# Two outer products of the first unit, M3 and M4, by two Strassen levels instead of one

## The chip, the cores and the metric

The kernel runs on one core of a Trainium2 chip. A core has a matrix engine (TensorE, "PE" in the profile, with its weight loads as "PEld"), a vector engine (VectorE, "DVE"), a scalar engine (ScalarE, "ACT"), a general engine (GpSimd, "POOL") and a queue engine (SyncE, "SP") that issues most transfers; 16 DMA engines move data. TensorE writes only to PSUM, which has eight banks here (tags `g1`, `g3`, `s0`, `s1`, `q01`, `q02`, `q11`, `q12`), each of 128 partitions by 512 numbers of float32. The metric is the time of one execution in microseconds (us), the median of several runs.

## The reference

The kernel computes a linear attention and feeds it to four experts whose results are summed by gates:

```python
# attention: 4 batches, 8 heads, 768 positions, 64 wide, in blocks of 64
intra = ((qb @ kb.T) * Dmask) @ vb
inter = (qb * lam_pow) @ kv_state
out[:, :, sl] = intra + inter
kv_state = lam_block * kv_state + (kb * rev_pow).T @ vb
...
x = attention_out                      # 3072 tokens x 512
p = domain_probs / (domain_probs.sum(-1, keepdims=True) + 1e-09)
for e in range(4):
    h = np.maximum(x @ w1[e], 0.0)     # 3072x512 @ 512x1024
    out += p[:, e:e + 1] * (h @ w2[e]) # 3072x1024 @ 1024x512
```

All is float32.

## The kernel before

The tokens are cut into three groups of 1024 (`g`), and a unit is one group with one expert, twelve in all. In each unit the first product `x @ w1[e]` and the second product `h @ w2[e]` are done by Strassen's scheme in Winograd's form: seven products M1 to M7 of sums of weight blocks (`A_OF`: A11, A12, A22 and the sums S1 to S4) with sums of token blocks (`B_OF`: B11, B21, B22 and T1 to T4). These seven are the outer products.

From the second unit on, each outer product of the first product is split once more by the same scheme (`first_product`): seven inner products of two matmul instructions, 128 x 256 each. For it the weight block is cut in four, and four inner sums (named S3, S1, S2, S4 again, `S_OPS`) are made by GpSimd into a tile `ops`; the token block is cut in four too, and four inner sums are made in place in `xs` (`x_steps`). The inner products go in the order M1, M7, M6, M4, M5, nothing, M3, M2 (`FIRST`). M1, M6, M5 and M3 add into one bank (`g1`), M7, M4 into another (`g3`), which is then taken anew for M2 and filled ahead with an earlier result by ScalarE (`seed`). After each of them VectorE or ScalarE reads the running sum out of the bank, adds what came earlier, and leaves a block of the result.

The first unit (group 0, expert 0) is different. Its token blocks come straight from the attention of group 0, which runs at the same time, and its outer products are done without the second split (`direct_product`, L1547 to L1585): four quarters of four matmul instructions, each quarter with a bank of its own. M6, M7 and M4 add into the same four banks (`chains`), so that M4's quarters hold M6 + M7 + M4. M7 and M4 need only a Relu after an addition of M5 and of M1. The order is M1, M2, M5, M6, M7, M3, M4 (`SEQ0`).

Since the inner weight sums of expert 0 are not used in the first unit, GpSimd makes them later, in the chores of `prepare_w1(0)`, and stores them in `w1_ops` in DRAM for groups 1 and 2, where `feed` loads them. The sums of expert 1, for the second unit, are made ahead of each outer product (`own_w1`), used from SBUF and stored too.

The order of the instructions on each engine is the order in which the program writes them. A planner decides on that: `now` counts steps of the main loop, `busy`, `moved`, `asked`, `filled` are its estimates of how far GpSimd, the DMA engines, SP and VectorE are booked. `pump` takes the next chore (`chores`: loads, weight sums) when these allow it, and sends stores (`queue`) some steps after their sums. `own_sums` holds VectorE's inner sums of the token blocks, of which one is taken at a step. An outer product that needs what has no entry yet makes the planner take it by force.

Tiles rotate: `stage` has seven buffers of 128 x 1024 for weight blocks and sums, `small` tiles of 128 x 512 come from a pool of 42. A tile that takes a used buffer waits for the last reader of that buffer. Each transfer signals on one of eight semaphores in turn, and one issued on a semaphore waits for the earlier one on it.

While M6, M7, M3 and M4 of the first unit run, VectorE also makes the sums of the token blocks (`x_sums`), the gates (`gates`, L578 to L600, four operations on VectorE and seven copies on ScalarE) and the inner sums of unit 1's first token block (`own_x("M1")`). The other inner sums of unit 1's token blocks are made in unit 1. GpSimd makes the sums of expert 0's and then expert 1's second weights (`prepare_w2`, tiles `w2b` and `w2o`), and the first weights of expert 1 (`w1b`, `w1o`, `ops`).

Of the kernel before, what the change touches and what calls it, by code (L numbers as in the profile page):

```python
# [12 lines left out]
ALU = mybir.AluOpType  # L13
# [8 lines left out]
def kernel(  # L22
# [233 lines left out]
    def weight_steps(block, total, ready):  # L256
        return [
            lambda: (block("A11", 0, 0), block("A21", 1, 0), block("A22", 1, 1)), pause(6),
            lambda: ready("M1"),
            lambda: total("S1", "A21", "A22", ALU.add), lambda: ready("M5"),  # L260
            lambda: total("S3", "A11", "A21", ALU.subtract), lambda: ready("M7"),
            lambda: (block("A12", 0, 1), total("S2", "S1", "A11", ALU.subtract)), lambda: ready("M6"),
            lambda: ready("M2"),
            lambda: total("S4", "A12", "S2", ALU.subtract), lambda: ready("M3"),
            lambda: ready("M4"),
        ]

    def prepare_w1(e):
        st = {}

        def block(name, i, j):
            t = stage.tile([P, 2, W], FP32, name="w1b", tag="st")
            src = moe_w1[e, j * 256:(j + 1) * 256, i * W:(i + 1) * W]
            send(out=t[:], in_=src.rearrange("(c p) f -> p c f", p=P))
            st[name] = t

        def total(name, a, b, op):
            t = stage.tile([P, 2, W], FP32, name="w1o", tag="st")
            halves(t[:], st[a][:], st[b][:], op)
            st[name] = t  # L280

        def ready(m):
            inner_w1(e, m, st[A_OF[m]])

        return weight_steps(block, total, ready)
# [768 lines left out]
    def first_product(g, e, m, blocks, tags):  # L1054
# [3 lines left out]
        while unit_of[g, e] in (1, 2 * E) and to_do.get(m):  # L1058
            take(own_sums, True)
# [444 lines left out]
    def own_w1(m):  # L1504

        c = w1_now[1][A_OF[m]]
        b = {f"A{i + 1}{j + 1}": c[j][:, i * 256:(i + 1) * 256] for i in range(2) for j in range(2)}
        s = stage.tile([P, 4, 256], FP32, name="ops", tag="st")
        for n, x, y, op in S_OPS:
            b[n] = s[:, SLOT[n]]  # L1510
            tt(nc.gpsimd, b[n], b[x], b[y], op)
        store(keep_own(("w1", 1, m), w1_ops[1, MS.index(m)], (
            ((0, 1), c[0][:, 0:256].unsqueeze(1)), ((1, 5), s[:]), ((5, 7), c[1].rearrange("p (a f) -> p a f", a=2)),
        )[slice(1, 2) if A_OF[m][0] == "A" else slice(0, 3)]))
        return {i: b[A_OF[i]] for i in A_OF}
# [8 lines left out]

    def own(m):
# [7 lines left out]
    ADDED = {"M1": None, "M2": "M1", "M5": "M1", "M6": "M5", "M7": "M5", "M3": "M6", "M4": "M1"}  # L1533

    def direct_product(m, blocks, tags):
# [4 lines left out]
        def quarter(at, part=None):  # L1540
# [4 lines left out]
            elif m in ("M2", "M6", "M7", "M4"):  # L1545
# [7 lines left out]
            for s in range(2) if part is None else (part,):  # L1553
                f = i * 256 + s * P
                for c in range(2):
                    nc.tensor.matmul(  # L1556
                        out=p[:, s * 256:(s + 1) * 256], lhsT=a[c][:, f:f + P], rhs=b[:, c, j * 256:(j + 1) * 256],
                        start=(s == 0 and c == 0 and m not in ("M2", "M7", "M4")), stop=True, skip_group_check=True,
# [4 lines left out]
            new[at] = blocks[old][at] if m in ("M7", "M3", "M4") else small("m" + at)  # L1563
# [7 lines left out]
            if m in ("M3", "M7", "M4"):  # L1571
                nc.scalar.activation(out=new[at][:], in_=new[at][:], func=AF.Relu)

# [81 lines left out]
    def sum_own(name, a, b, op=ALU.subtract):  # L1655
# [14 lines left out]
    for m in SEQ0[2:]:  # L1670
# [3 lines left out]
        work = direct_product(m, blocks, ("g1", "g3")) if m != "M5" else [m5[1], *m5[3:]]  # L1674
# [38 lines left out]
    for at, (g, e) in enumerate(units):  # L1713
# [15 lines left out]
        for i in range(7):  # L1729
# [36 lines left out]
            if at == i == 0:  # L1766
                for m in SEQ[1:]:
                    own_x(m)
# [73 lines left out]
```

## Time and profile before

The time before is 1155.02 us, the median of three runs (1154.9 to 1155.08).

| what | value |
|---|---|
| profiled execution, its own time | 1158.15 us |
| its span, first to last instruction | 1156.3 us |
| TensorE clock granted | 1.000 |
| TensorE busy | 1143.0 us (99%) |
| VectorE busy | 790.0 us (68%) |
| ScalarE busy | 369.8 us (32%) |
| GpSimd busy | 771.4 us (67%) |
| data moved | 269.22 MB, 233 GB/s |
| first unit's M6 and M7 on TensorE | 59.88 to 73.84 us |
| first unit's M3 | 73.84 to 80.75 us |
| first unit's M4 | 80.75 to 87.65 us |
| second unit's first matmul | 87.65 us |

A row of a group of instructions gives: line, engine, operation, tiles written <- tiles read, shape, count | busy time in us, mean time of one in ns | idle time of the engine just before them and what ended it. A row in order of time gives: start in us, length in us, engine, line, operation, tiles, shape, count, and in brackets the idle time before and what ended it. In a table of stretches a row gives the stretch, its length, then for PE, PEld, DVE, ACT and POOL the busy us and the count, the TensorE clock, the busy share of the DMA engines and GB/s. In the chain, a row is start, length and what the chain went through. The line of nearly every tensor_tensor operation is that of a helper (L117), so the tiles tell which it is: `pc` and `pM` are banks of the first unit's direct products, `pg` of two-level products, `q` of second products, `m` are blocks of results, `xs` token blocks, `ops` inner weight sums, `w1o` and `w2o` outer weight sums, `w1b` and `w2b` raw weight blocks. TensorE runs a float32 matmul instruction as two records.

### The profile page before, as it was taken

The page shows a single profiled execution, that of the slowest core. Times are in us where ns is not written, and L with a number is a line of the kernel's source. Part 1 is how long each engine was busy: PE and PEld are TensorE (multiplying, and loading weights), DVE is VectorE, ACT ScalarE, POOL GpSimd, SP SyncE. Part 2 cuts the span into 40 slices and gives each one's busy share as a digit, 9 for nine tenths or more (in the row PEclk, how much of TensorE's full clock was granted, in tenths as well). Part 3 has the DMA queues.
Part 4 walks back from the last instruction along what each step waited for, and adds up shares of the span by engine and source line. Part 5 has one row for each costly group of instructions (what it writes and reads, how often), then busy time and mean ns, then how long its engine had stood idle before and what let it go on. Part 6 is the DMA issues. An engine that isn't in the chain of part 4 may idle for free.

```text
span 1156.3 us, 22167 instructions
## 1 busy us (share of the span) xinstructions
PE 1143.0 (99%) x8015; PEld 990.3 (86%) x8015; DVE 790.0 (68%) x1428; ACT 369.8 (32%) x746; POOL 771.4 (67%) x732
## 2 busy tenths in 40 slices
PE   8999999999999999999999999999999999999998
PEld 7788888888888888888888888888888888888887
DVE  5576775477477757835775567989765566776785
ACT  4322133223312221222243442243354442342332
POOL 2748318647742974874784998894995783873884
PEclk9999999999999999999999999999999999999999
DMA  8796667999899999895957669966777756657552
GB/s 192 175 281 190 175 191 230 310 292 285 280 302 315 275 287 300 268 349 178 296 186 243 193 201 284 311 226 203 219 241 248 219 167 198 195 162 210 171 191 74
DMA packets 309148, 269.22 MB, mean 233 GB/s; under 512 B 141424, under 2 KB 244016, under 8 KB 309040
## 3 DMA queue, kind: packets, MB, share of 16 engines
q1 hardware_dynamic: 291360, 262.66, 74.0%
q10 hardware_dynamic: 17648, 5.15, 2.0%
q8 instruction: 64, 1.05, 0.4%
q14 instruction: 44, 0.36, 0.1%
q0 software_dynamic: 32, 0.00, 0.0%
HBM read 194.83 MB, written 77.10 MB: 235 GB/s over the span
## 4 chain that ended last, share of the span: by engine, by line
PE 87%; DVE 5%; POOL 3%; issue 1%; DMA 1%; SPq 1%; ACT 1%; DVEq 0%; POOLq 0%; ACTq 0%
PE pg L1096 37%; PE pq L1454 20%; PE q L1155 20%; DVE m L117 2%; PE pM L1556 2%; PE pc L1556 2%; POOL acc L117 1%; DVE sums L117 1%; PE sp L721 1%; PE op L775 1%; POOL ops L117 1%; DVE xs L117 1%; PE sp L728 1%; PE op L793 1%; SPq L114 1%
## 5 line engine op out<-in xcount | busy, mean ns | idle before, releaser
L1096 PE MATMUL pg<-xs,ws_in 128*128 128x256 f32 x1960 | 473.0, 381 | 3.7 <-DVE m L117 3.5
L1096 PEld LDWEIGHTS pg<-xs,ws_in 128*128 128x128 f32 x1960 | 369.0, 190 | 59.5 <-DVE m L117 9.5
L117 DVE TENSOR_TENSOR m<-pg,m 128x512 f32<-128x512 f32 x374 | 255.4, 686 | 104.1 <-PE pg L1096 92.0
L1155 PE MATMUL q<-w2t,m 128*128 128x256 f32 x1120 | 265.7, 380 | 0.5 <-DVE m L117 0.5
L1155 PEld LDWEIGHTS q<-w2t,m 128*128 128x128 f32 x1120 | 212.1, 190 | 29.9 <-DVE m L117 1.1
L117 POOL TENSOR_TENSOR m<-m,decay 128x512 f32<-128x512 f32 x91 | 115.4, 1283 | 89.4 <-ACT m L1113 74.0
L117 DVE TENSOR_TENSOR sums<-pq,sums 128x256 f32<-128x256 f32 x272 | 112.9, 421 | 85.5 <-PE pq L1454 75.8
L1454 PE MATMUL pq<-acc,w2t 128*128 128x256 f32 x688 | 169.3, 379 | 0.0
L1454 PEld LDWEIGHTS pq<-acc,w2t 128*128 128x128 f32 x688 | 130.7, 190 | 17.8
L1113 ACT ACTIVATE m<-m 128x512 f32<-128x512 f32 x99 | 62.4, 630 | 191.2 <-DVE m L117 191.0
L117 DVE TENSOR_TENSOR m<-m,m 128x512 f32<-128x512 f32 x112 | 103.4, 923 | 6.0 <-ACT m L1079 5.9
L1173 DVE SCALAR_TENSOR_TENSOR acc<-q,gate,acc 128x256 f32<-128x256 f32 x108 | 52.0, 481 | 73.9 <-PE q L1155 73.7
L1109 ACT COPY m<-pg 128x512 f32<-128x512 f32 x88 | 51.6, 586 | 123.8 <-PE pg L1096 119.4
L1073 ACT COPY pg<-m 128x512 f32<-128x512 f32 x77 | 45.4, 589 | 133.3 <-DVE m L117 118.7
L117 POOL TENSOR_TENSOR acc<-hT,hT 128x512 f32<-128x512 f32 x56 | 71.2, 1287 | 18.2 <-PE pq L1454 15.7
L117 POOL TENSOR_TENSOR acc<-hT,acc 128x512 f32<-128x512 f32 x56 | 71.3, 1273 | 8.5 <-PE pq L1454 4.7
L1454 PE MATMUL pq<-hT,w2t 128*128 128x256 f32 x288 | 70.0, 379 | 0.0
L117 POOL TENSOR_TENSOR w2o<-w2b 128x512 f32<-128x512 f32 x26 | 35.5, 1386 | 49.0 <-DMA w2b<-in_moe_w_dram 44.5
L1454 PEld LDWEIGHTS pq<-hT,w2t 128*128 128x128 f32 x288 | 54.5, 190 | 7.6
L1454 PE MATMUL pq<-m,w2t 128*128 128x256 f32 x228 | 55.5, 380 | 0.0
L928 ACT COPY hp<-m 128x512 f32<-128x512 f32 x84 | 48.4, 589 | 16.0 <-DVE hT L117 15.0
L117 POOL TENSOR_TENSOR xs<-xs 128x256 f32<-128x256 f32 x28 | 23.8, 849 | 44.5 <-DMA xs<-x_blocks 42.8
(149 smaller groups left out, 1438.4 us busy)
## 6 DMA issues: line engine op xcount, KB each, us to landing
w2t<-w_ops SPq DMA_DIRECT2D x129, 256.0 KB, 3.4
ws_in<-w_ops SPq DMA_DIRECT2D x40, 512.0 KB, 4.8
ws_in<-w_ops SPq DMA_DIRECT2D x60, 256.0 KB, 3.9
ws_in<-w_ops SPq DMA_DIRECT2D x40, 384.0 KB, 4.7
w2b<-in_moe_w_dram SPq DMA_DIRECT2D x56, 256.0 KB, 5.3
w_ops<-ops SPq DMA_DIRECT2D x28, 512.0 KB, 4.7
w2t<-w_sums SPq DMA_DIRECT2D x40, 256.0 KB, 4.5
w_sums<-w2o SPq DMA_DIRECT2D x16, 512.0 KB, 4.6
```

The costliest lines, as they stand in the source:

```text
L114: (by or nc.sync).dma_start(out=out, in_=in_)
L117: eng.tensor_tensor(out=o, in0=a, in1=b, op=op)
L721: nc.tensor.matmul(out=sp[r][half[x], ac * BL:(ac + 1) * BL], lhsT=hc(kT)[half[r], ac, blk[x]], rhs=hc(qT)[half[r], ac, blk[x]], start=(ac ...
L928: nc.scalar.copy(out=there[x][:], in_=blk[at][:])
L1073: nc.scalar.copy(out=banks[tags[1]][:], in_=new["11"][:])
L1096: nc.tensor.matmul(out=p[:, j * 256:(j + 1) * 256], lhsT=ws[i][:, j * P:(j + 1) * P], rhs=xs[i], start=(fresh and j == 0), stop=True, skip ...
L1109: nc.scalar.copy(out=new[at][:], in_=p[:])
L1113: nc.scalar.activation(out=new[at][:], in_=new[at][:], func=AF.Relu)
L1155: nc.tensor.matmul(out=p[:, s * DH:(s + 1) * DH], lhsT=h[A_OF[m]][:, c * 256 + s * P:c * 256 + (s + 1) * P], rhs=fed2[g, e, m][uu][:, c], ...
L1173: nc.vector.scalar_tensor_tensor(out=o, in0=x, scalar=w, in1=o, op0=ALU.mult, op1=ALU.add)
L1454: nc.tensor.matmul(out=p[:, 0:256], lhsT=fed3[e, m, x // 2][:, x % 2, c * P:(c + 1) * P], rhs=b[B_OF[i]][:, c * 256:(c + 1) * 256], start= ...
L1556: nc.tensor.matmul(out=p[:, s * 256:(s + 1) * 256], lhsT=a[c][:, f:f + P], rhs=b[:, c, j * 256:(j + 1) * 256], start=(s == 0 and c == 0 an ...
```

## The change

M3 and M4 of the first unit are now done by `first_product`, with two levels. Their inner weight sums are made early by `own_w1(m, 0)`, called through `first_ops` from two new chores and from the main loop, into `small` tiles (two of four halves each instead of one `stage` tile), and stored to `w1_ops` from there. `prepare_w1(0)` leaves out S4, M3 and M4 in return. The inner sums of the two token blocks are made by VectorE during M7 and M3 (`own_x("M3")`, `own_x("M4")`) and no longer in unit 1; `own_x("M1")` moves to the end of M3, and the gates move from the end of M6 to M4. So that `first_product` finds what it adds to, M7 now also adds its banks onto M1's blocks (four more VectorE operations), and M6's and M1's blocks are handed over as U4 and U3.

```diff
-    def weight_steps(block, total, ready):
+    def weight_steps(block, total, ready, all_of=True):
...
+        ] + ([
             lambda: total("S4", "A12", "S2", ALU.subtract), lambda: ready("M3"),
             lambda: ready("M4"),
-        ]
+        ] if all_of else [])
...
-        return weight_steps(block, total, ready)
+        return weight_steps(block, total, ready, e != 0)
...
-        while unit_of[g, e] in (1, 2 * E) and to_do.get(m):
+        while unit_of[g, e] in (0, 1, 2 * E) and to_do.get(m):
...
-    def own_w1(m):
+    def own_w1(m, e=1):
 
-        c = w1_now[1][A_OF[m]]
+        c = w1_now[e][A_OF[m]]
...
+        if e:
+            s = [stage.tile([P, 4, 256], FP32, name="ops", tag="st")[:]]
+        else:
+            s = [small("ops")[:].rearrange("p (a f) -> p a f", a=2) for _ in range(2)]
...
+    def first_ops(m):
+        if (0, 0, m) not in fed:
+            fed[0, 0, m] = own_w1(m, 0)
...
-            if m in ("M3", "M7", "M4"):
+            if m == "M7":
                 nc.scalar.activation(out=new[at][:], in_=new[at][:], func=AF.Relu)
+                tt(nc.vector, blocks["M1"][at][:], p[:], blocks["M1"][at][:], ALU.add)
...
-        ("M6", 3): (lambda: x_sums(("T4", 1)), gates), ("M3", 1): (lambda: own_x("M1"),),
+        ("M6", 3): (lambda: x_sums(("T4", 1)), lambda: own_x("M3")), ("M7", 3): (lambda: own_x("M4"),),
+        ("M3", 3): (lambda: own_x("M1"),), ("M4", 1): (gates,),
...
     chores.extend((
+        lambda: first_ops("M3"), lambda: first_ops("M4"),
         lambda: own_weights("M1"), sum_own("S1", "A21", "A22", ALU.add), *w2_steps[0:4], mine["M1"], *w2_steps[4:],
...
-        work = direct_product(m, blocks, ("g1", "g3")) if m != "M5" else [m5[1], *m5[3:]]
+        if m in ("M3", "M4"):
+            first_ops(m)
+            blocks["U4"], blocks["U3"], blocks["left"] = blocks["M6"], blocks["M1"], 0
+            a = first_product(0, 0, m, blocks, ("g1", "g3"))
+            work = [lambda fs=fs: [f() for f in fs if f] for fs in (a[0:2], a[2:4], a[4:6], a[6:8], a[8:])]
+        else:
+            work = direct_product(m, blocks, ("g1", "g3")) if m != "M5" else [m5[1], *m5[3:]]
...
-                for m in SEQ[1:]:
+                for m in SEQ[1:5]:
                     own_x(m)
```

More of the change, by code (lines that the diff above doesn't have):

```diff
@@ L1502, in own_x @@
         own_sums.extend(after(wait, f) for f in steps)
-    def own_w1(m):
-        c = w1_now[1][A_OF[m]]
+    def own_w1(m, e=1):
+        c = w1_now[e][A_OF[m]]
         b = {f"A{i + 1}{j + 1}": c[j][:, i * 256:(i + 1) * 256] for i in range(2) for j in range(2)}
-        s = stage.tile([P, 4, 256], FP32, name="ops", tag="st")
+        if e:
+            s = [stage.tile([P, 4, 256], FP32, name="ops", tag="st")[:]]
+        else:
+            s = [small("ops")[:].rearrange("p (a f) -> p a f", a=2) for _ in range(2)]
+        w = 4 // len(s)
         for n, x, y, op in S_OPS:
-            b[n] = s[:, SLOT[n]]
+            b[n] = s[SLOT[n] // w][:, SLOT[n] % w]
             tt(nc.gpsimd, b[n], b[x], b[y], op)
-        store(keep_own(("w1", 1, m), w1_ops[1, MS.index(m)], (
-            ((0, 1), c[0][:, 0:256].unsqueeze(1)), ((1, 5), s[:]), ((5, 7), c[1].rearrange("p (a f) -> p a f", a=2)),
-        )[slice(1, 2) if A_OF[m][0] == "A" else slice(0, 3)]))
+        made_of = [((1 + w * x, 1 + w * x + w), t) for x, t in enumerate(s)]
+        raw_of = ((0, 1), c[0][:, 0:256].unsqueeze(1)), ((5, 7), c[1].rearrange("p (a f) -> p a f", a=2))
+        store(keep_own(
+            ("w1", e, m), w1_ops[e, MS.index(m)],
+            made_of if A_OF[m][0] == "A" else [raw_of[0], *made_of, raw_of[1]],
+        ))
         return {i: b[A_OF[i]] for i in A_OF}
@@ L1532 @@
     chains, CHAIN = {}, {"11": "q01", "12": "q02", "21": "q11", "22": "q12"}
-    ADDED = {"M1": None, "M2": "M1", "M5": "M1", "M6": "M5", "M7": "M5", "M3": "M6", "M4": "M1"}
+    ADDED = {"M1": None, "M2": "M1", "M5": "M1", "M6": "M5", "M7": "M5"}
     def direct_product(m, blocks, tags):
@@ L1544, in quarter @@
                 p = opened.pop((m, at))
-            elif m in ("M2", "M6", "M7", "M4"):
+            elif m in ("M2", "M6", "M7"):
                 if m == "M6":
@@ L1557, in quarter @@
                         out=p[:, s * 256:(s + 1) * 256], lhsT=a[c][:, f:f + P], rhs=b[:, c, j * 256:(j + 1) * 256],
-                        start=(s == 0 and c == 0 and m not in ("M2", "M7", "M4")), stop=True, skip_group_check=True,
+                        start=(s == 0 and c == 0 and m not in ("M2", "M7")), stop=True, skip_group_check=True,
                     )
@@ L1562, in quarter @@
                 return
-            new[at] = blocks[old][at] if m in ("M7", "M3", "M4") else small("m" + at)
+            new[at] = blocks[old][at] if m == "M7" else small("m" + at)
             blocks[m] = new
```

## The prediction

> **What bounds the kernel now.** I read the page's busy shares first, then its chain that ended last, then the waits of TensorE, and last the lists in order of time between 56 and 104 us, where the change sits. From the page:
>
> ```profile
> PE 1143.0 (99%) x8015; PEld 990.3 (86%) x8015; DVE 790.0 (68%) x1428; ACT 369.8 (32%) x746; POOL 771.4 (67%) x732
> PE 87%; DVE 5%; POOL 3%; issue 1%; DMA 1%; SPq 1%; ACT 1%; DVEq 0%; POOLq 0%; ACTq 0%
> L1096 PE MATMUL pg<-xs,ws_in 128*128 128x256 f32 x1960 | 473.0, 381 | 3.7 <-DVE m L117 3.5
> ```
>
> TensorE is busy 99% of the span, and its largest group waits 3.7 us in the whole kernel. So every matmul taken out is time gained, every new TensorE wait is time lost, and nothing later can give a loss back: there is no idle time to absorb it. The chain in order of time shows the two products that change:
>
> ```profile
> 73.84 6.91 PE pM L1556 x32
> 80.75 6.91 PE pc L1556 x32
> 87.65 1.73 PE q L1155 x8
> ```
>
> One product is 32 matmul records (16 instructions of two records) in 6.91 us: 0.216 us a record.
>
> **Part 1, TensorE.** A one-level product has 16 matmul instructions, a two-level one 7 inner products of 2, so 14. Two products lose 4 instructions, 8 records: 8 x 0.216 = -1.73 us. That is all the change can win; it is 0.15%, and 0.2% (2.3 us) is about what a measurement of this kernel tells from no change.
>
> **Part 2, VectorE before M3 and inside M3 and M4.** Direct M3 and M4 read out a finished bank four times, and TensorE goes to another bank meanwhile. Two-level ones alternate between two banks, g1 and g3, and each inner product adds onto what its bank holds, so TensorE may write a bank only after VectorE has read it. In unit 1, eight records of the second product lie between the pairs of inner products; in the first unit nothing does. The rows for VectorE:
>
> ```profile
> 63.51 0.68 DVE L117 TENSOR_TENSOR m<-pc,m 128x512 f32<-128x512 f32 x1
> 64.11 0.68 DVE L117 TENSOR_TENSOR xs<-xs,b 128x512 f32<-128x512 f32 x1
> 74.48 1.44 DVE L117 TENSOR_TENSOR m<-m,m 128x512 f32<-128x512 f32 x1
> 77.94 0.41 DVE L117 TENSOR_TENSOR xs<-xs 128x256 f32<-128x256 f32 x1
> L117 DVE TENSOR_TENSOR xs<-xs 128x256 f32<-128x256 f32 x12 | 7.7, 644 | 0.1
> ```
>
> The first four are in order of time, the last is a group of 97.7 to 114 us. Back to back, VectorE starts a 128x512 operation every 0.60 us. With both inputs in SBUF it is slower beside GpSimd: the 128x256 subtraction takes 0.41 us while POOL rests and 0.64 on average while POOL works, so I add 0.23: 0.33 + 0.23 = 0.56 us from start to start, and 0.83 for a 128x512 one (its other end is the 1.44 above).
>
> POOL rested from 62.5 to 68.2 us; the change fills that time (part 3). From 63.51 us on, VectorE has before M3's first read-out: 12 reads from PSUM (4 of M6, 4 of M7, and the 4 new sums of M7 onto M1) at 0.60 = 7.2; four subtractions of x and the S3 of hid, 128x512, at 0.83 = 4.15; five 128x256 subtractions for M3's and M4's x (moved here from unit 1) at 0.56 = 2.8. The gates (1.71 us, from 68.31 to 70.02) leave this stretch. Sum 14.15, so the read-out of M3's first bank starts at 77.66 and ends at 78.35. TensorE did its first two inner products from 73.84 to 75.57 and waits: 2.85 us. Without GpSimd beside it the same list, now held up by M7's last matmul at 73.77, lets TensorE go at 76.75 (1.2 us); at 0.83 and 1.2 us an operation it goes at about 81 (5.3 us). I take 2.85, since POOL works here in 128x256 steps, as in the group shown.
>
> Inside a product M1, M7, M6, M4, M5 then take turns with 0.86 us each against 0.69 of reading, which covers. M3 comes straight behind M5 on the same bank, and the empty slot between them is filled in unit 1 alone: 0.77 (0.69 and the way there and back) to 1.0 us, I take 1.0 for M3, where VectorE has a subtraction in hand. M4's second inner product waits until ScalarE has read M3's last bank, behind two Relus of 0.63: 0.25. The next S3 on VectorE waits for that Relu and holds up M4's first read-out: 0.5. The gates now stand behind M4's fourth inner product and, with one subtraction (0.33), ahead of the read-out of M5: 1.71 + 0.33 + 0.69 less 0.2 that is covered = 2.5 us. (ScalarE's seven gate copies, 0.85 us from 70.13, go ahead of M4's seed copy; that ends before the last inner product needs it and costs nothing, or 0.6 if the gates run later.) Waits 2.85 + 1.0 + 0.25 + 0.5 + 2.5 = 7.1, less 1.73: unit 1 begins 5.4 us late (3.5 to 8 with the ends above).
>
> **Part 3, GpSimd, SP and the DMA engines.** In the built order `first_ops` runs twice for M3 and twice for M4: the main loop makes the sums and takes them out of `fed` at once, the two chores come later, find no entry and make them again, with their stores. So POOL gets 16 operations of 128x256 instead of 8, and SP 12 stores: twice 128 + 3x256 KB for M3, twice 2x256 KB for M4, 2.88 MB. These rows are POOL's and the DMA's (start, length; the third fence line is from the table of stretches):
>
> ```profile
> 56.60 5.85 POOL L117 TENSOR_TENSOR w2o<-w2b,w2o 128x512 f32<-128x512 f32 x4
> 68.17 0.80 POOL L117 TENSOR_TENSOR ops<-w1b 128x256 f32<-128x256 f32 x1 [5.73 <-DMA w1b<-in_moe_w_dram]
> 74.00:88.00 14.00, 14.00 (x67) 12.34 (x66) 9.20 (x15) 5.04 (x8) 4.24 (x4) 1.00 0.98 312
> 82.09 2.87 POOL L117 TENSOR_TENSOR w2o<-w2b 128x512 f32<-128x512 f32 x2 [6.71 <-DMA w2b<-in_moe_w_dram]
> 89.49 2.68 POOL L117 TENSOR_TENSOR w2o<-w2b 128x512 f32<-128x512 f32 x2 [4.53 <-DMA w_sums<-w2o]
> 92.25 5.38 POOL L117 TENSOR_TENSOR w2o<-w2b,w2o 128x512 f32<-128x512 f32 x4
> 97.70 1.72 POOL L117 TENSOR_TENSOR ops<-w1o 128x256 f32<-128x256 f32 x2
> 103.05 1.03 PE L1096 MATMUL pg<-xs,ops 128*128 128x256 f32 x4
> ```
>
> M3's sums start at 62.45, long before TensorE asks; 16 x 0.79 puts unit 1's M1 sums to about 78, asked for at 90. What is late is M5 of unit 1. Its sums were begun at 97.70 and its first is read at 103.05, and they stand on POOL behind the four sums of w2 of expert 1, which start when the w2b blocks land (82.09). The DMA engines are 98% busy there at 312 GB/s, so the stores push the blocks back. Ahead of the blocks now also go two w2t loads, one 512 KB store and four small copies: 1.18 MB. Together 4.06 MB / 312 GB/s = 13.0 us; by the steps in which transfers landed there (0.64 us for a 256 KB store, 0.35 for 128 KB, 1.25 for 512 KB, 0.8 for a 256 KB load, 0.2 for a copy) 10.75. I take 12: the second copies wait on SP for the first to land. So w2o starts at 94.1, and the chain from there to the first M5 sum stays as shown, 82.09 to 98.6 = 16.5 us: 110.6. (A new wait of the third w2 sum, for the last matmul that reads unit 1's M1 sums, falls at 104.6 and is as late as the chain itself.) TensorE, 5.4 us late, asks at 108.45 and waits 2.15 us. M6, M2 and the later products of unit 1 had 8 to 16 us of slack on POOL; the chain is about 12 late, TensorE 7.5, so they still hold.
>
> **Part 4, what goes later.** Expert 0's own chores lose one weight sum (2 x 1.36) and 8 inner sums (8 x 0.79), 9 us of POOL, and four stores. POOL is 67% busy and TensorE's later waits sum to a few us, so this gains between 0 and 1 us; I take 0. The re-ordered chores could add a wait: up to 1 us, 0 taken.
>
> Sum: 5.4 + 2.15 = 7.55 us. The profiled execution took 1158.15 us (span 1156.3), 3.13 over the median of the runs; I put the difference onto the median: 1155.02 + 7.55 = 1162.6, range of this case 1160.6 to 1164.1.
>
> [...]
>
> **Rivals.**
> - *The cover holds, not slower.* If VectorE reads M3's first bank by 75.57, the read-outs inside keep up and the w2b blocks land by about 86, only -1.73 is left: 1153.3, within 0.2%. For it: 0.69 of reading against 0.86 of matmuls. Against it: 14.15 us of VectorE work in a stretch of 12. It decides at the wait of M6 in M3. Chance 0.05.
> - *The transfers are hidden.* The w2b blocks land by 92, M5's sums come in time and only part 2 counts: 1160.4 (1158.5 to 1161). For it: the lower estimate, 10.75. Chance 0.21.
> - *The transfers cost more.* 15 us instead of 12, for SP's waits on the first copies: 1165.6. Chance 0.12.
> - [...] Chance 0.10.
>
> **The numbers.** My case has 0.48, the rest (0.04) is unforeseen, half of it past the range. The range 1158.4 to 1167.5 holds all but the first rival and that. Faster by over 0.2% would need more than the matmuls give: 0.02. Within 0.2%: 0.05. Slower: 0.93.
>
> **What would show it.** In the profile after: M3 and M4 as 56 records of `pg` with 128x256; a TensorE wait of 2 to 4 us near 75.6 put down to VectorE's `m`, one of about 2.5 us near 89 behind the gates; the first `q` of unit 1 at 92 to 95 instead of 87.65; 16 `ops` operations on POOL from 62.5 without a rest; `w2o<-w2b` of expert 1 at 93 to 95; a wait for POOL `ops` of about 2 us in unit 1's M5, near 108. From 130 us on both kernels should run alike, shifted. Wrong if VectorE is not behind at 75.6, or if later stretches differ by more than 1 us.

## The result, and the profile after

The changed kernel takes 1167.96 us (median of 5 runs, 1166.83 to 1172.44) against 1155.08 us before: 1.0118 times as long, with an interval of 1.0097 to 1.0139. It is slower, as forecast, by 12.9 us instead of 7.5, and 0.46 us above the forecast's range. The profiled execution took 1167.96 us too, with a span of 1166.2 us and a mean TensorE clock of 0.997. The two profiled executions differ by 9.8 us only, because M3 begins at 71.25 us in the one of the changed kernel and at 73.67 us in the other; in the kept traces it begins anywhere from 71.25 to 75.45 us. So the traces are compared from M3's first matmul on.

The page of the changed kernel, busy shares and the largest group:

```profile
PE 1144.7 (98%) x8007; PEld 988.4 (85%) x8007; DVE 788.3 (68%) x1436; ACT 371.5 (32%) x748; POOL 778.3 (67%) x738
L1097 PE MATMUL pg<-xs,ws_in 128*128 128x256 f32 x1960 | 472.8, 381 | 2.9 <-DVE m L117 2.7
```

TensorE has its 8 records less (8007 for 8015), the largest group waits no more than before (2.9 us for 3.7), and yet TensorE is busy for 1.7 us more. The rest is in one place. The changed kernel's TensorE in order of time (start, length, and in brackets the idle time before it and what ended it):

```profile
71.25 1.03 PE L1097 MATMUL pg<-xs,w1o 128*128 128x256 f32 x4
72.11 1.03 PE L1097 MATMUL pg<-xs,ops 128*128 128x256 f32 x4
75.74 1.10 PE L1097 MATMUL pg<-xs,ops 128*128 128x256 f32 x4 [2.60 <-DVE m L117]
79.76 1.10 PE L1097 MATMUL pg<-xs,ops 128*128 128x256 f32 x4 [1.01 <-DVE m L117]
88.99 1.10 PE L1097 MATMUL pg<-xs,ops 128*128 128x256 f32 x4 [1.76 <-DVE m L117]
90.80 0.38 PE L1156 MATMUL q<-w2t,m 128*128 128x256 f32 x1
...
110.34 2.08 PE L1097 MATMUL pg<-xs,ops 128*128 128x256 f32 x4 [3.84 <-POOL ops L117]
112.21 3.58 PE L1156 MATMUL q<-w2t,m 128*128 128x256 f32 x8
115.62 1.03 PE L1097 MATMUL pg<-xs,ops 128*128 128x256 f32 x4
```

The first five lines are taken from M3 and M4 and show their three longest waits for VectorE; the sixth is unit 1's first `q`. From M3's first matmul to it are 19.55 us, against 13.82 us before (64 records of 0.216). The line behind the dots is the wait for the sums of unit 1's M5: 19.54 us from the first `q` to it, against 15.56 us before (87.49 to 103.05). The eight matmuls at 112.21 then take 3.41 us from start to start (to 115.62), where before such eight took 1.73 us. The table of stretches (length, busy us and count of TensorE, weight loads, VectorE, ScalarE and GpSimd, TensorE's clock, DMA share, GB/s) says why:

```profile
105.50:110.30 4.80, 1.00 (x5) 0.54 (x3) 2.78 (x3) 0.59 (x1) 4.80 (x6) 0.84 0.76 274
110.30:116.00 5.70, 5.66 (x14) 4.56 (x15) 0.18 (x1) 0.59 (x1) 5.54 (x7) 0.53 0.94 256
116.00:121.00 5.00, 5.00 (x25) 4.40 (x24) 4.05 (x7) 1.18 (x2) 4.84 (x6) 1.00 0.36 74
```

Behind the wait TensorE runs at a clock of 0.53: 14 records in 5.7 us, 0.427 us from start to start instead of 0.216. It has its full clock again from 115.6 us on. From the first `q` to the turning of k and q at 161.87 us (151.76 before) the kernel takes 71.08 us, against 64.28 before: 3.98 us is the wait (19.54 less 15.56), the other 2.8 us the half clock. So 5.7 + 4.0 + 2.8 = 12.5 us lie between M3 and that point, and the rest, 1004.3 us to the end against 1004.6, runs as before.

GpSimd in the changed kernel, on the way to that wait:

```profile
95.66 2.67 POOL L117 TENSOR_TENSOR w2o<-w2b 128x512 f32<-128x512 f32 x2 [13.35 <-DMA w2b<-in_moe_w_dram]
101.31 2.86 POOL L117 TENSOR_TENSOR w2o<-w2b 128x512 f32<-128x512 f32 x2 [2.98 <-DMA w_sums<-w2o]
104.13 5.47 POOL L117 TENSOR_TENSOR w2o<-w2b,w2o 128x512 f32<-128x512 f32 x4
109.57 1.40 POOL L117 TENSOR_TENSOR ops<-w1o 128x256 f32<-128x256 f32 x2
```

and SP's queue, where the w2 blocks are asked for:

```profile
74.25 3.49 SPq L114 DMA_DIRECT2D w_ops<-w1o  x2
...
84.51 2.93 SPq L114 DMA_DIRECT2D across<-in_k_dram  x2
87.48 1.07 SPq L114 DMA_DIRECT2D w2t<-w_sums  x2
88.60 0.43 SPq L114 DMA_DIRECT2D w_ops<-ops  x1
89.08 1.71 SPq L114 DMA_DIRECT2D w2b<-in_moe_w_dram  x2
```

GpSimd is idle for 13.35 us for the w2 blocks. SP asked for them at 89.08 us instead of 76.15; counted from M3's first matmul (71.25 here, 73.67 before) that is 15.4 us later.

### The profile page after: what moved, and what is told of

It is laid out like the page before. It is cut to its first block, busy times and chain, and to the rows that moved or that the text cites. A ratio compares the mean times of both kernels' runs of the same rounds, so it can differ in the third digit from the quotient of the medians.

```text
span 1166.2 us, 22172 instructions
## 1 busy us (share of the span) xinstructions
PE 1144.7 (98%) x8007; PEld 988.4 (85%) x8007; DVE 788.3 (68%) x1436; ACT 371.5 (32%) x748; POOL 778.3 (67%) x738
## 4 chain that ended last, share of the span: by engine, by line
PE 90%; DVE 7%; issue 1%; POOL 1%; DMA 1%; ACT 0%; DVEq 0%; POOLq 0%; ACTq 0%
PE pg L1097 39%; PE pq L1455 22%; PE q L1156 20%; DVE m L117 3%; PE pM L1568 2%; DVE xs L117 1%; PE sp L722 1%; PE op L776 1%; DVE sums L117 1%; PE op L794 1%; PE sp L729 1%; PE qp L692 1%; POOL w2o L117 1%; PE kp L692 1%; PE pg L1455 0%
## 5 line engine op out<-in xcount | busy, mean ns | idle before, releaser
L117 DVE TENSOR_TENSOR m<-pg,m 128x512 f32<-128x512 f32 x386 | 264.0, 687 | 108.8 <-PE pg L1097 97.8
L1114 ACT ACTIVATE m<-m 128x512 f32<-128x512 f32 x105 | 66.3, 632 | 201.7 <-DVE m L117 195.1
L117 DVE TENSOR_TENSOR m<-m,m 128x512 f32<-128x512 f32 x112 | 96.5, 862 | 7.3 <-ACT m L1080 7.3
L1110 ACT COPY m<-pg 128x512 f32<-128x512 f32 x88 | 51.7, 587 | 130.9 <-PE pg L1097 126.5
L1078 ACT COPY m<-pg 128x512 f32<-128x512 f32 x44 | 25.8, 587 | 83.3 <-PE pg L1097 83.3
```

The lines of the kernel that those rows point to most:

```text
L117: eng.tensor_tensor(out=o, in0=a, in1=b, op=op)
L1078: nc.scalar.copy(out=o[:], in_=p[:])
L1110: nc.scalar.copy(out=new[at][:], in_=p[:])
```

## The experiments

The stage is measured in each trace from M3's first matmul to the turning matmul near 155 us ("the stage" below, 78.1 us before, 90.6 after; with one-level products M3's begin is put 13.82 us ahead of the first `q`). Ratios are to the kernel before on the same chip, where it took 1155.98 to 1157.84 us. In `seeded`, `seeded_before`, `read_first_seeded` and `inner_order` part of what ScalarE puts into a bank is missing from the sums; which, is told in the last section. Their instructions are whole.

### Half of the sums and stores, and a wait in the kernel before

`once` makes the sums and stores of M3 and M4 once, `sums_twice` keeps the second sums and leaves out the second stores (the edit of `once`):

```diff
+    firsts = set()
     def first_ops(m):
-        if (0, 0, m) not in fed:
+        if m not in firsts:
+            firsts.add(m)
             fed[0, 0, m] = own_w1(m, 0)
```

> Edit: the sums of M3 and M4 are made and stored once each; all else as in the changed kernel. Theory A (the changed kernel lost 5.7 us in M3 and M4 of the first unit, 4 us at the M5 sums of unit 1, and 3 us because TensorE ran at half clock after that wait): the first-unit loss stays, so the second product of unit 1 starts as late as before, but six stores and the stops of SP behind them are gone and the w2b blocks land 6 to 9 us earlier. The M5 sums then wait not for the blocks but for the last matmul that reads the M1 sums of unit 1 (their buffer is taken by a w2 sum): 2 to 3 us instead of 3.8, and the granted clock stays 1.00 or drops if 2.6 us is already enough. Time 1163.5 us (1163 to 1166.5). Rival B (the transfers alone made the M5 sums late): no wait at M5, 1160.8. Rival C (the loss lies in the second level itself, nothing in the copies): 1167.5 to 1168.5.

> Edit: the sums of M3 and M4 are still made twice on GpSimd, but stored once. Theory A: GpSimd's 6.4 us are idle time anyway (it waited 13.35 us for the w2b blocks in the changed kernel), the transfers alone made the M5 sums late, so this equals the kernel that makes and stores once: 1163.5 us, within 1 us of it. Rival D (GpSimd's time counts): as the changed kernel, 1167 to 1168.

`once` took 1171.62 us, 1.0123 (1.0105 to 1.0140), `sums_twice` 1171.1 us, 1.0113 (1.0096 to 1.0130): no gain from either, where some 4 us had been expected. They equal each other, so the second sums on GpSimd cost nothing by themselves. GpSimd in `once`:

```profile
92.46 2.95 POOL L117 TENSOR_TENSOR w2o<-w2b 128x512 f32<-128x512 f32 x2 [16.32 <-DMA w2b<-in_moe_w_dram]
98.43 2.50 POOL L117 TENSOR_TENSOR w2o<-w2b 128x512 f32<-128x512 f32 x2 [3.01 <-DMA w_sums<-w2o]
104.75 2.66 POOL L117 TENSOR_TENSOR w2o<-w2b,w2o 128x512 f32<-128x512 f32 x2 [3.82 <-issue]
109.75 2.48 POOL L117 TENSOR_TENSOR w2o<-w2b,w2o 128x512 f32<-128x512 f32 x2 [2.34 <-DMA w2b<-in_moe_w_dram]
112.19 1.40 POOL L117 TENSOR_TENSOR ops<-w1o 128x256 f32<-128x256 f32 x2
```

The blocks come 4.8 us sooner after M3's begin (19.65 us instead of 24.41), but two other waits take the gain. The third w2 sum needs, by the program, the stage buffer of unit 1's M1 sums and starts 12.4 us after unit 1's first `q` (92.36), when the last matmul that reads them is through. The profile names no releaser for it; but it starts 12.38 or 12.39 us after that `q` in four more traces (`stores_late`, `m5_once_gates`, `seeded`, `read_first`). And the last w2 block is asked for on SP only behind two w2t loads, which wait for `q` matmuls (4.4 us on SP), so it lands at 109.6. The wait for M5's sums is 4.91 us, and the half clock follows. Two limits lie at nearly the same time; halving the one shows the other.

`hold10` and `hold12` put 10 and 12 more 128x256 subtractions on GpSimd ahead of M5's sums in the kernel *before*:

```diff
+        if m == "M5":
+            for _ in range(10):
+                nc.gpsimd.tensor_tensor(out=s[:, SLOT["S3"]], in0=b["A11"], in1=b["A21"], op=ALU.subtract)
```

> Edit: the kernel before, with ten more subtractions of 128x256 on GpSimd just ahead of the M5 sums of unit 1, each written over by the real one later. GpSimd was 4.4 us ahead of TensorE there; ten cost 7.0 to 7.7 us, so TensorE waits 2.6 to 3.3 us. Theory A (the loss at M5 is the wait, plus a half clock only when the wait is long enough; waits of 2.6 and 1.8 us in the changed kernel gave no half clock): 1157.7 to 1158.4 if the clock holds, 3 us more (1161) if 3 us is enough to lose it. Rival E (the slow matmuls after the wait in the changed kernel have another cause, such as late weights or the DMA load): full clock whatever the wait, 1158.

> Edit: the kernel before, with twelve more subtractions there instead of ten. The wait is 4.0 to 4.9 us. Theory A: the matmuls after it take 0.427 us from start to start instead of 0.216 for 3 to 5 us, as in the changed kernel, so the loss is the wait and 2 to 3 us more: 1161.5 to 1163. Rival E: full clock after the wait, 1159 to 1160.

They took 1164.19 us, 1.0052 (1.0037 to 1.0067), and 1164.4 us, 1.0061 (1.0045 to 1.0078). The waits were 4.87 and 5.50 us, longer than expected; in `hold10` the w2 blocks also came 0.9 us later, counted from M3's begin, than in the trace of the kernel before. TensorE in `hold10`:

```profile
108.36 2.08 PE L1096 MATMUL pg<-xs,ops 128*128 128x256 f32 x4 [4.87 <-POOL ops L117]
110.23 2.49 PE L1155 MATMUL q<-w2t,m 128*128 128x256 f32 x8
```

From `q` to the turning the kernel lost 6.6 and 7.45 us, 1.6 and 1.8 us more than the 5.0 and 5.7 us by which M5 began late. So the half clock is not the change's own: a late sum brings it in the old kernel too.

### Are the waits of M3 and M4 and the late sums one loss or two?

`early_direct` has the changed kernel's early sums, stores and order on GpSimd and SP, but multiplies M3 and M4 by one level (the diff is the removed lines of `direct_product` and `sums_then` put back). `gates_late` moves the gates behind M4's last read-outs:

```diff
-        ("M3", 3): (lambda: own_x("M1"),), ("M4", 1): (gates,),
+        ("M3", 3): (lambda: own_x("M1"),), ("M4", 3): (gates,),
```

> The kernel before, with the changed kernel's early sums and stores of M3's and M4's weights (made twice, as there) and its order on POOL and SP, but with M3 and M4 multiplied by one level as before; nothing is left out. Theory A (the late chain on SP and POOL is enough by itself, and the waits of M3 and M4 lie beside it): unit 1 starts as in the kernel before, the wait for M5's sums is 8 to 10 us, the half clock follows it, and the time is 1166 to 1168.5 us, nearly the changed kernel's. Theory B (the waits add up): the wait is 3.8 us as in the changed kernel, with the half clock, and the time is 1161.5 to 1162.5 us.

> The changed kernel, with the gates' operations behind M4's last read-outs instead of ahead of them; nothing is left out. Theory A (the time at which M5's sums come is set by SP and POOL alone, so the waits in M3 and M4 lie beside it): the wait of 1.8 us ahead of M5 of M4's inner products goes, unit 1 starts 1.8 us earlier, and the wait for M5's sums grows by as much, from 3.8 to 5.6 us: 1168.0 us, within 0.7 of it. Theory B (the waits add up, as the prediction had them): 1166.2 us, and the wait for M5's sums stays at 3.8 us.

Theory A holds in both, though both times lie above its ranges; the kernel before took 1157.64 us on this chip, and by the ratio both are as slow as the changed kernel. `early_direct` took 1169.86 us, 1.0100 (1.0069 to 1.0131). Its M3 and M4 wait for nothing, and TensorE's waits from 70 to 118 us are one:

```profile
PE pg L1097 <- POOL ops L117: 11.0, 1, 11.0
```

`gates_late` took 1170.23 us, 1.0105 (1.0074 to 1.0135). The wait ahead of M5 fell from 1.76 to 0.88 us, and the one for the sums grew:

```profile
PE pg L1097 <- POOL ops L117: 5.8, 1, 5.8
PE pg L1097 <- DVE m L117: 4.3, 4, 2.4
```

The time at which M5's sums come sets the end of the stage, and what is lost earlier only shortens the wait for them. (The expectation calls adding the waits up "as the prediction had them"; the prediction's own sum was that of an end time, 110.6 us, so it agrees with theory A.)

### Taking the late sums away

`m5_early` makes M5's sums right after S1, ahead of the w2 sums, in two small tiles. `m5_once_gates` is this with the edits of `once` and `gates_late`:

```diff
-        if e:
+        if e and m != "M5":
             s = [stage.tile([P, 4, 256], FP32, name="ops", tag="st")[:]]
...
-        lambda: own_weights("M1"), sum_own("S1", "A21", "A22", ALU.add), *w2_steps[0:4], mine["M1"], *w2_steps[4:],
+        lambda: own_weights("M1"), sum_own("S1", "A21", "A22", ALU.add), lambda: own_weights("M5"), *w2_steps[0:4], mine["M1"], *w2_steps[4:],
```

> The changed kernel, with the four sums of unit 1's M5 made right after S1, ahead of the w2 sums, and kept in two small tiles instead of a stage buffer; nothing is left out. Theory A (what follows the first unit is lost at one wait, for M5's sums behind the late w2 chain, and the half clock after it): both go, 3.84 us of wait and some 2.9 us of half clock less, and what is left is the 5.7 us of M3 and M4: 1161.2 us, between 1160 and 1162.5; no stretch of matmuls at 0.43 us. Theory B (the first w2 chain is late for everything behind it, and M6's sums take the place of M5's): a wait of 2 to 5 us for POOL's sums some 29 us after unit 1's first q, and 1164 to 1168 us.

> The changed kernel with three edits: M5's sums ahead of the w2 sums, the sums and stores of M3 and M4 made once, the gates behind M4's read-outs; nothing is left out. Theory A: only the waits of M3 and M4 for VectorE are left, 2.6 and 1.0 us and some tenths, less 1.7 us of matmuls that the two levels save, with no half clock: 1157.5 to 1159.5 us. [...]

1165.25 us, 1.0066 (1.0044 to 1.0088), and 1163.64 us, 1.0049 (1.0035 to 1.0062). In both, the wait for POOL's sums and the half clock behind it are gone, and from the first `q` on the stage takes 64.26 us, as before. No later sum took its place. But both are slower than theory A had it, in part because the kernel before took 1157.64 us on this chip for 1155.08. In the traces the stage still loses 6.9 and 6.6 us, since the wait at M3's M6 (2.05 and 3.15 us) now brought a half clock of its own, 1.3 us. In the other executions that need not be so: two of `m5_early`'s seven had a granted clock of 1.000 and took 1164.99 and 1165.25 us, no less. The time of `m5_once_gates` lies 4.1 us above theory A's range; what VectorE loses beside GpSimd is taken up below.

`stores_late` takes `early_direct` and issues the 12 stores behind the w2 blocks and sums:

```diff
-        store(keep_own(
+        (store if e else kept.append)(keep_own(
...
         lambda: own_weights("M1"), sum_own("S1", "A21", "A22", ALU.add), *w2_steps[0:4], mine["M1"], *w2_steps[4:],
+        lambda: [f() for f in kept],
```

> The kernel with the early sums and with M3 and M4 by one level, whose wait for M5's sums is 11.0 us, with the twelve stores of those sums issued behind unit 1's w2 blocks and w2 sums instead of ahead of them; POOL's 16 early operations stay, nothing is left out. Theory A (the stores hold SP, and so the w2 blocks, back): the w2 blocks are asked for some 6 us or more earlier, and the wait for M5's sums falls to 0 to 3 us: 1157 to 1161.5 us. Theory B (the second set of sums on POOL makes the chain late): the wait stays over 7 us and the time over 1164 us.

1166.46 us, 1.0075 (1.0055 to 1.0094). The wait fell from 11.0 to 3.8 us, neither A's 3 or less nor B's 7 or more. GpSimd in `stores_late`:

```profile
85.51 1.28 POOL L117 TENSOR_TENSOR w2o<-w2b 128x512 f32<-128x512 f32 x1 [4.14 <-DMA w2b<-in_moe_w_dram]
...
99.66 2.67 POOL L117 TENSOR_TENSOR w2o<-w2b,w2o 128x512 f32<-128x512 f32 x2 [5.58 <-issue]
103.57 2.48 POOL L117 TENSOR_TENSOR w2o<-w2b,w2o 128x512 f32<-128x512 f32 x2 [1.25 <-DMA w2b<-in_moe_w_dram]
106.01 1.40 POOL L117 TENSOR_TENSOR ops<-w1o 128x256 f32<-128x256 f32 x2
```

So the stores' place on SP is worth 7.2 us of the 11.0 of wait. What is left is what `once` showed: the third w2 sum starts 12.4 us after `q` (87.27) again, behind M1's matmuls, although its blocks have long landed. The second set of sums on GpSimd is not needed to explain anything. How much of the 7.2 us is SP standing still and how much the stores' bytes on the DMA engines, these runs do not separate.

### What M3's M6 waits for

The prediction laid this wait to VectorE's work list of 14.15 us. In the changed kernel VectorE indeed worked without a pause from M6's first read-out to M3's first, 13.82 us (first and last lines of it):

```profile
61.09 0.68 DVE L117 TENSOR_TENSOR m<-pc,m 128x512 f32<-128x512 f32 x1
...
73.42 0.43 DVE L117 TENSOR_TENSOR xs<-xs 128x256 f32<-128x256 f32 x1
73.78 1.21 DVE L117 TENSOR_TENSOR m<-m,m 128x512 f32<-128x512 f32 x1
74.91 1.27 DVE L117 TENSOR_TENSOR m<-pg,m 128x512 f32<-128x512 f32 x2
```

The last two operations ahead of the read-out take 1.49 us of it (73.42 to 74.91). `seeded` takes eight 128x512 additions out of that list: ScalarE copies M1's blocks into the chain's four banks ahead of M6.

```diff
+    for at in CHAIN:
+        chains[at] = bank(CHAIN[at], "pc")
+        nc.scalar.copy(out=chains[at][:], in_=blocks["M1"][at][:])
...
-            if old is None:
+            if old is None or m == "M5":
                 nc.scalar.copy(out=new[at][:], in_=p[:])
...
-                tt(nc.vector, blocks["M1"][at][:], p[:], blocks["M1"][at][:], ALU.add)
+                nc.scalar.copy(out=blocks["M1"][at][:], in_=p[:])
```

> The kernel with M5's sums first, the sums and stores made once and the gates late, and with VectorE relieved of eight 128x512 additions: ScalarE copies M1's blocks into the four banks of the chain ahead of M6, so that M6 and M7 add onto them, M5's blocks are copied out without M1, and the sum of M1, M6 and M7 is a copy of the bank. Nothing is left out. Theory A (M3's M6 waits for VectorE's work list of some 14 us): the list is 8 times 0.60 us, 4.8 us, shorter where M3 begins, the wait of 3.2 us falls under 0.5 us, no matmul runs at 0.43 us, and the other waits stay at 0.9 to 1 us each: 1156.5 to 1158.5 us beside 1163.6 of the kernel without the seeds and 1157.6 of the kernel before. Theory B (the wait is that of the two banks and their read-outs in turn, whatever lies ahead on VectorE): the wait stays over 2 us and the time at 1161 to 1164 us.

> The kernel before with the seeds alone: the four banks of the chain are seeded with M1's blocks by ScalarE, M5's blocks are copied out without M1, and M4's blocks are the Relu of the bank, 8 additions less on VectorE; nothing is left out. Theory A (nothing in the kernel before waits for VectorE in this stage): no change, 1156.8 to 1158.3 us beside 1157.6 of the kernel before. Theory B (the seeds are a gain or a loss of their own, by the banks that they need early): over 2 us to either side.

`seeded_before` made no difference, 0.9998 (0.9985 to 1.0012), as A had it. `seeded` took 1161.43 us, 1.0035 (1.0022 to 1.0047), where `m5_once_gates` had 1.0049, but in its trace, taken in the slowest of its eleven executions (1164.82 us), the wait at M6 stayed 2.46 us, against theory A. VectorE in `seeded`:

```profile
74.83 0.69 DVE L117 TENSOR_TENSOR m<-pc,m 128x512 f32<-128x512 f32 x1 [0.58 <-PE pc L1568]
75.44 1.13 DVE L117 TENSOR_TENSOR xs<-xs 128x256 f32<-128x256 f32 x1
76.49 1.75 DVE L117 TENSOR_TENSOR m<-m,m 128x512 f32<-128x512 f32 x1
78.16 1.27 DVE L117 TENSOR_TENSOR m<-pg,m 128x512 f32<-128x512 f32 x2
```

VectorE is no longer behind: it waited for M7's last matmuls. The read-out at 78.16 stands behind a subtraction for M4's x and the operand sum of M7's blocks, 2.7 us together, which nobody waits for. Beside GpSimd they took 1.13 and 1.75 us; the same shapes take 0.41 and 0.69 us in the kernel before, at 77.94 and 81.72. So the wait is behind these two, and 1.8 us of them is VectorE held back beside GpSimd. `read_first` moves these two, in M3 and in M4, behind the first read-outs (on `m5_once_gates`; `read_first_seeded` on `seeded`):

```diff
-        ("M6", 3): (lambda: x_sums(("T4", 1)), lambda: own_x("M3")), ("M7", 3): (lambda: own_x("M4"),),
-        ("M3", 3): (lambda: own_x("M1"),), ("M4", 3): (gates,),
+        ("M6", 3): (lambda: x_sums(("T4", 1)), lambda: own_x("M3")),
+        ("M3", 0): (lambda: own_x("M4"),), ("M4", 0): (lambda: own_x("M1"),), ("M4", 3): (gates,),
...
-            rest()
+            if (m, x) not in (("M7", 4), ("M3", 4)):
+                rest()
```

> The kernel with M5's sums first, the sums and stores made once and the gates late, and with two pieces of VectorE's work moved from ahead of the first read-outs of M3 (and of M4) to behind them: the operand sum of M7's (M3's) blocks and the first weightless sum of the next outer product's right side; nothing is left out. Theory A (M3's M6 waits for what stands directly ahead of its read-out on VectorE, 1.05 and 1.67 us beside the second sum in the trace of the seeded kernel): the wait of 3.2 us falls to 0.3 to 1.6 us, no matmul runs at 0.43 us, and the time is 1159 to 1161 us beside 1163.6. Theory B (VectorE's whole work list since M5 sets it): the wait stays over 2.3 us, and the time within 1 us of 1163.6.

> The same with the seeds, eight additions less on VectorE. The sums of this kernel are not the reference's: part of what ScalarE copies into the banks is not in what the matmuls leave there; instructions and their order are whole, and only the times are read. Theory A: no wait over 0.3 us at M3's M6, and the other waits as they were, 0.87, 0.11, 0.23 and 0.88 us, against 1.7 us of matmuls less: 1157 to 1159 us, the kernel before within 1 us. Theory B: 1160.5 to 1162 us, as with the seeds alone.

In `read_first` the wait at M6 fell from 3.15 to 1.16 us, no half clock followed, and M3 to `q` took 18.03 us instead of 20.41; a new wait of 0.66 us came inside M3, behind the two operations moved there. The profile lays the 1.16 us to a GpSimd sum; but M3's first read-out ran from 75.83 us, straight behind M7's, to 76.5, and TensorE went on at 76.65, so this rest of the wait is VectorE's list. With the seeds the wait at M6 is 0.01 us, but one of 1.74 us stands in its place: 18.04 us again. The times were 1163.34 us, 1.0050 (1.0036 to 1.0063), and 1163.05 us, 1.0047 (1.0032 to 1.0063): not what A expected of them, though the stages were. That called for the same kernels beside each other.

### One chip, and the waits taken out one by one

`read_first_again` and `m5_once_gates_again` are the same kernels once more. `inner_order` changes `read_first`: M2 of the inner products gets a bank of its own, filled by ScalarE during M4, and stands between M5 and M3; M4's outer product begins on the other bank.

```diff
-            a = first_product(0, 0, m, blocks, ("g1", "g3"))
+            a = first_product(0, 0, m, blocks, ("g1", "g3", "s0") if m == "M3" else ("g3", "g1", "s1"))
...
-        return [i and (lambda i=i: inner(i)) for i in FIRST] + [lambda: finished(g, e, m, blocks, new)]
+        return [i and (lambda i=i: inner(i)) for i in (FIRST if len(tags) < 3 else ("M1", "M7", "M6", "M4", "M5", None, "M2", "M3"))] + [lambda: finished(g, e, m, blocks, new)]
```

> read_first with the inner products of M3 and M4 in another order and on other banks: M2, on a bank of its own that ScalarE fills during M4, stands between M5 and M3, and M4's outer product begins on the bank that M3 did not end on; nothing is left out. Theory A (each wait that goes from M3 and M4 is time gained, once M5's sums are early): the two waits of 0.87 and 0.88 us and the one of 0.11 go, the others stay (1.16, 0.66 and 0.40 us), the stretch from M3 to unit 1's first q is 16 us instead of 18.0, and the time is 2 us under that of read_first on this chip. Theory B (the end of the stage is set by something else, as a time of 1163.3 us instead of 1160 for read_first would have it): the stretch is shorter, the time within 0.7 us of read_first's.

> read_first once more, on the same chip as the kernel without its edit. Theory A: from M3 to q 18.0 us again, 2 us or more less time than the kernel beside it. Theory B: 18.0 us again, but a time within 0.7 us of the other's.

> The kernel that read_first was made from, once more, on the same chip: 20.4 us from M3 to q in the trace before, of which 1.3 us are matmuls at 0.43 us behind the wait of 3.2 us. Theory A: 2 us or more above read_first's time. Theory B: within 0.7 us of it; if the half clock does not show this time, the stretch is 19.1 us.

In that order 1160.64 us, 1.0021 (1.0008 to 1.0034); 1162.04 us, 1.0036 (1.0024 to 1.0049); and 1164.12 us, 1.0060 (1.0041 to 1.0079). M3 to `q` took 15.79, 17.41 and 19.21 us. The medians follow the stages (2.1 us for 1.8, 1.4 us for 1.6), as A had it, but the intervals overlap. The first run of `read_first` was 6.5 us above the kernel before with a stage only 4.2 us longer; these 2 us stay unexplained.

`inner_banks` uses two of the chain's banks for M2 (`q01` and `q02` for `s0` and `s1`), and `inner_rest` moves the operand sums behind the fourth pair of inner products:

```diff
-            if (m, x) not in (("M7", 4), ("M3", 4)):
+            if (m, x) != ("M7", 4) and (m not in ("M3", "M4") or x == 3):
```

> inner_order with M2's own bank taken from the four of the chain, which M6 and M7 have written in full, instead of those of the attention; nothing is left out. Theory A (the time follows the stretch from M3 to q): 15.8 us from M3 to q again, 2.0 us more than in the kernel before, and a ratio to it of 1.001 to 1.003. Theory B (a chain bank is late, or its copy is): a wait of over 0.5 us for ScalarE's copy or for the bank, and 1.004 or more.

> inner_banks with VectorE's operand sums of the blocks behind the fourth pair of inner products of M3 and M4 instead of behind the first; nothing is left out. Theory A (only what stands ahead of a read-out on VectorE counts): the waits of 0.66 and 0.41 us at M5 of the inner products go or halve, 14.8 to 15.3 us from M3 to q, a ratio of 1.000 to 1.002: still not faster than the kernel before. Theory B (VectorE's whole load counts): the waits come back at M3 or in M4, 15.8 us or more, and 1.002 or more.

`inner_banks`: 1159.13 us, 1.0031 (1.0019 to 1.0044), 15.40 us from M3 to `q`. `inner_rest`: 1158.36 us, 1.0022 (1.0013 to 1.0030), 15.91 us. TensorE's waits from 70 to 118 us in `inner_banks`, then in `inner_rest` (total, times, longest):

```profile
PE pg L1097 <- DVE m L117: 1.6, 3, 0.6
```

```profile
PE pg L1097 <- DVE m L117: 2.2, 2, 1.8
```

In `inner_rest` the waits inside M3 and M4 all but went, and 1.8 us came back at M3's M6 (0.6 in `inner_banks`). The numbers are theory B's, but the edit did not bring this wait: VectorE's order ahead of that read-out is the same in both kernels. The same list, from M6's first read-out to the last two of M7, took 10.62 us in `inner_banks` and 12.91 in `inner_rest`, where a subtraction of M3's x took up to 0.98 us beside GpSimd. So how VectorE's list falls beside GpSimd's sums is worth over 1 us from one trace to the next.

With these waits moved, M3 and M4 by two levels still take 15.4 us and more against 13.8 by one; 12.1 us would be their matmuls alone. Some 1.7 us of the difference stand in no row of the waits. In the changed kernel inner products without a listed wait begin 0.93 to 0.95 us apart instead of 0.86, and a listed wait costs 0.2 to 0.3 us more from start to start than its row says. That takes back the 1.73 us that two levels save; why, no run here shows. By the ratios these versions are some 10 and 11 us faster than the changed kernel, and neither is faster than the old one.

## Why the prediction was right and where it was wrong

The forecast was 5.4 us for part 2 and 2.15 us for part 3; the trace has 5.7 us, 4.0 us and, with no term in the forecast, 2.8 us of half clock. Two steps failed: the landing of the w2 blocks, taken at 12 us, and the clock, taken at nothing without a word.

- *Part 1* holds: 56 records of `pg`, 12.09 us without waits, 1.73 less than 13.82.
- *Part 2, sum:* near, and partly by luck. Unit 1 starts 5.73 us late, 5.4 forecast. The waits are 2.60, 1.01, 0.11, 0.23 and 1.76 us where 2.85, 1.0, 0.25, 0.5 and 2.5 were forecast, 1.4 us less in all; small delays between the inner products, 1.75 us, which the forecast did not have, make up for it.
- *Part 2, cause of the first wait:* right in the changed kernel, as far as it goes. "VectorE has before M3's first read-out" a list of 14.15 us, said the step; it was 13.82 us without a pause. The step did not see that the order inside the list counts: by the rows, 1.49 us of the 2.60 are two operations at its end that nobody waits for, and the other 1.1 us the backlog (1.16 in `read_first`, where the two stand behind). Nor does a shorter list help as long as these two stand there: in `seeded` the list was held up by M7's last matmuls, as the step itself had it for a list without GpSimd beside it, and the wait stayed.
- *Part 3, mechanism:* right. The early stores push the w2 blocks back, the chain on GpSimd from the blocks to M5's sums is as long as before or shorter (14.7 us; 16.5 forecast), and its end sets the stage (`early_direct`, `gates_late`).
- *Part 3, size:* the failed term is "I take 12" for the landing of the blocks. GpSimd's first w2 sum began 24.41 us after M3's begin, and 8.42 us before: 16 us later. SP stands still for 4.3 us of that, until stores have landed (below; with the stores made once, `once`, SP waits for none of them there); the rival at 15 us for this had 0.12. With the shorter chain, M5's sums came 39.1 us after M3's begin; the forecast's 110.6 is 36.9. The wait was 3.84 us for 2.15. SP's waits in the changed kernel from 74 to 90 us (total, times, longest):

```profile
SPq L114 <- DMA w_ops<-w1o: 2.7, 2, 2.6
SPq L114 <- DMA w_ops<-ops: 1.6, 4, 0.6
```

- *The term that was missing:* the clock. No step asked at what clock TensorE goes on after a wait. It costs 2.8 us here, more than the whole wait as forecast, and 1.3 to 3.4 us in the experiments. In the trace the clock changes in steps of 3.41 us (last section), and the wait of 3.84 us lay with 2.28 and 1.56 us in two of them: the clock fell at the end of the first, in which TensorE was still busy for 1.13 us. By the steps of this case each of the forecast waits of 2.85 and 2.15 us could have cost something, if 2.05 us or more of it fell into one step.
- *The buffer:* the remark that a wait for M1's matmuls "is as late as the chain itself" holds: it is one of the two reasons why halving the sums and stores gained nothing.
- *Part 4* holds: 1004.3 us from the turning on, against 1004.6.

With 16 us for the blocks and 14.7 for the chain, M5's sums would have come at 82.09 + 30.7 = 112.8 us, 4.3 after TensorE asks (108.45); 5.4 + 4.3 = 9.7 us, and with the clock 12.5. The loss measured is 12.9 us.

## What to carry to other kernels

Before a store or a sum is made early, find what stands behind it on its queue and which chain starts there: here 12 stores on SP cost 7 us of wait on GpSimd's sums two products later. Where one chain's end sets a stage, waits ahead of it cost nothing and taking them out gains nothing, until the chain is cut; cut it first, then count. And on an engine that runs at 99%, price a wait of 2 us or more with the slower clock that may follow it (half, for 3.4 to 10.2 us here), and put read-outs that free a bank ahead of every sum that has time.

## What the runs showed of the hardware

- *The granted clock fell and rose in steps of 3.41 us.* In the changed kernel's trace it is 1.00 for 102.400 us, 0.50 for 6.827 us and 1.00 for 1051.305 us: 30, 2 and 308 steps of 3.413 us. In all traces it changes only at multiples of this from its first change, and the thirteen stretches of half clock between M3 and 122 us last one, two or three steps. The steps of the changed kernel (length, busy us and count of TensorE, weight loads, VectorE, ScalarE and GpSimd, clock, DMA share, GB/s):

```profile
105.37:108.78 3.41, 1.13 (x6) 0.65 (x4) 2.78 (x3) 0.59 (x1) 3.41 (x4) 1.00 0.99 360
108.78:112.19 3.41, 1.85 (x4) 1.51 (x5) 0.00 (x0) 0.00 (x0) 3.25 (x5) 0.50 0.61 212
112.19:115.61 3.42, 3.42 (x9) 2.70 (x8) 0.00 (x0) 0.59 (x1) 3.42 (x4) 0.50 0.95 229
115.61:119.02 3.41, 3.41 (x17) 3.01 (x16) 2.25 (x4) 1.18 (x2) 3.25 (x5) 1.00 0.58 122
```

  A fall came at the end of every step at full clock in which TensorE was idle for 2.05 us or more (twelve, 2.05 to 3.41) and of one with 1.76; steps with 1.79, 1.80 and 1.88 us of idle time had none. The clock came back at the end of the first step with 0.6 us or less of idle time; seven steps with 1.56 us and more stayed at half. So a wait's place on the steps counts beside its length. All eight waits of 3.8 us and more (3.81 in `stores_late` to 11.0 in `early_direct`) brought a fall; of eight between 2.05 and 3.28 us, four did (2.05, 2.06, 2.46 and 3.15, not 2.37, 2.60, 2.74 and 3.28: the 3.28 us were split into 1.40 and 1.88).
- *The price of a fall was about half of the half clock that was left when the wait ended.* From the first `q` to the turning, less the wait, it was 2.8, 1.7, 1.6 and 1.8 us in the changed kernel, `early_direct`, `hold10` and `hold12`; 5.3, 3.3, 3.1 and 3.5 us of half clock were left there. It did not grow with the wait (3.84, 11.0, 4.87 and 5.50 us). `stores_late` is off by 0.8 us: 3.4 us behind 3.81 of wait, with 5.2 left.
- *What ScalarE put into a bank was lost in part where the attention's smaller matmuls had used the bank, and kept where M6 and M7 had written it in full.* `inner_order` and `inner_banks` differ in the bank that ScalarE fills for M2 alone; with one that the attention's smaller matmuls had used, the outputs are off by 0.056, with one that M6 and M7 had written in full no seed is lost. The four seeds of `seeded` and `seeded_before`, in banks that the attention used as well, are off by 0.055. Why, these runs do not show.
- *An addition of two SBUF inputs on VectorE took longer beside a GpSimd sum.* In the kernel before, the 45 `m<-m,m` of 128x512 that no GpSimd operation overlapped took 0.65 to 0.69 us, the 67 others 0.68 to 1.81 us, 1.09 in the mean; `m<-pg,m`, with one input in PSUM, took 0.65 to 0.69 us in both cases (103 and 271). `m<-m,m`, 128x512, began at 76.49 in `seeded`, 0.25 us after a 128x512 sum on GpSimd (76.24 to 77.69), and ended at 78.24, 0.55 us after that sum's end, 1.75 us long. In `read_first` it began at 77.02, 0.18 us before a 128x256 sum on GpSimd ended (77.20), took 0.73 us, and GpSimd's next sum 1.06 instead of 0.72. In these two rows the length went with the time that GpSimd's operation still had to go, 1.20 us in the one and 0.18 in the other; the prediction's 0.64 us for a 128x256 subtraction is an average over such cases.
